# Second batch's softmax sums and joined maxima computed by PE, and the weights' sign written as a byte by GpSimd

## The chip, the cores and the metric

The kernel runs on one core of one Trainium2 chip. A core has five engines that run their own instruction streams side by side: PE (TensorE, matrix products into PSUM), DVE (VectorE, elementwise work, reductions, 32x32 transposes), ACT (ScalarE, functions such as exp and ln), POOL (GpSimd, elementwise work in SBUF, no PSUM) and SP (SyncE, which here only issues DMAs). The metric is the device time of one launch in microseconds (us); lower is better.

## The reference

Attention with 32 global and 512 local tokens for 8 batches of 8 heads (head size 64), and behind it a feed-forward layer on all 8 x 544 rows. Each local query sees the 32 global keys and the local keys at most 32 places away; each global query sees all keys.

```python
s_g = scale * np.matmul(q_g, k_all.transpose(0, 1, 3, 2))
out_g = np.matmul(sm(s_g), v_all)
mask = np.abs(pos[:, None] - pos[None, :]) <= window
s_ll = np.where(mask, scale * np.matmul(q_l, k_l.transpose(0, 1, 3, 2)), -1e9)
out_l = np.matmul(sm(np.concatenate([s_lg, s_ll], axis=-1)), v_all)
x = attn_out.transpose(0, 2, 1, 3).reshape(B * S, H * D)      # 4352 x 512
h = x @ w_in                                                   # 512 x 2048
g = np.maximum(h, 0.0) + np.log1p(np.exp(-np.abs(h)))
out = g @ w_out                                                # 2048 x 512
```

`sm` is the softmax: the row's maximum is subtracted, the exponentials are divided by their sum plus 1e-9. All inputs are fp32, but the weights come as 64-bit words: on the host the float32 array is viewed as `uint64` only, and the program gets them as pairs of 32-bit words, of which it works out a float32 value per pair.

## The kernel before

**Numbers of the feed-forward layer.** Every operand is split into two float32r halves (a rounded value and the rest), and each product is done three times (high x high, high x low, low x high), by `hpart` (h = x w_in, four pairs of heads j, 16 blocks f of 128 columns) and `opart` (o = g w_out). All products go through the helper `mm` (line 132), which chains them: PE executes them in the order in which the program writes them. `act` (lines 530 to 537) turns h into g: three ACT functions, a DVE instruction (L533) that reads the PSUM tile a last time, a rounded copy on ACT (L536, `gh`), the rest on POOL (L537, `gl`).

**Weights.** There are 16 blocks each of w_in and w_out. `load_w` brings a block as pairs of words, low and high. `abs_w` (L470, ACT) scales the value of the high word as a float, `bits_w` builds the float32 on DVE with three instructions: L477 shifts that left by three, L479 masks the sign out of the high word and ors it in, L482 shifts the low word right by 29 and ors. `halves_w` (L487 on ACT, L488 on POOL) splits it into two float32r tiles. Nine blocks are done during the first batch's attention, in which the order of DVE and ACT is written out by hand (`keep`, `note`): a block's three DVE instructions stand between a step's row maximum (L169, L170) and the inverse of its sums (L178, L179). The others follow in the next stage, each behind the latest joined maxima on DVE (`after(i, "maxima")`); `weights` takes one block whole before the next. Most of the temporary tiles of these steps share the tag "mb" with the attention's spread maxima, two buffers.

**Attention.** The first batch (m = 0 to 3, two heads each) is done by queries, in ten steps, before the feed-forward layer starts. All later batches go by keys: pair m computes score products with keys as rows (`scores`, two parts p, each into a two-bank PSUM tile), and each query's maximum and sum run across partitions. For the second batch (m = 4 to 7, `m < MPE`) PE adds the mask and ACT copies the scores (L310); later DVE does both (L312). DVE's transposing reduction L313 leaves for each 32-row block a column of maxima, and `gather` joins the four blocks: three POOL copies (L325) bring them to partitions 0 to 31, four DVE reductions and a copy (L328 to L332) join them by query, three more copies (L338) send them back. `probs` spreads the maxima by a DVE transpose (L346), POOL subtracts them in place (L355, L357), and ACT takes the exponential (L358). `sums` does the same with additions (L368, `gather`, L371 to L377), and `values` multiplies by the values on PE and by the inverse sums on DVE (L396).

**Order around the change.** A list of pieces, each with a place in the program, is mixed into the feed-forward layer's products: for pair m, scores at 12m and 12m+6 (with the maxima and exponentials behind the second), sums at 12m+14, values at 12m+21. In the first batch's products the 54 places from 54 to 108 are spread over the products by their count. Outside the hand-written part a planner orders each engine's instructions but PE's, by the program's order and estimated times.

**PSUM.** Tag "a" is one tile of two banks for scores, value products and the first batch's transposes; tag "h" is two banks for h; the rest holds o (before that, the first scores).

```python
ps.append((12 * m + 8 + LAG_Z, lambda m=m: sums(m)))      # LAG_Z = 6
def end(m):
    return 12 * m + 8 + LAG_V                             # LAG_V = 13
```

Of the kernel before, what the change touches and what calls it, by code (L numbers as in the profile page):

```python
# [35 lines left out]
LAG_V = 13  # L36
STEP = 3
# [26 lines left out]
def moe_over_global_local_attention(  # L64
# [27 lines left out]
    identf = pl.tile([P, P], F32, tag="e", name="identf", bufs=2)  # L92
    mask = const.tile([P, 2, 512], BF16, name="mask")
# [14 lines left out]
    def key_masks():  # L108
        near = mask[:, 1]
# [207 lines left out]
    def grid(t, start, *dims):  # L317
        base = t[0:32, start:start + 1]
        return bass.AP(base.tensor, base.offset, [list(base.ap[0])] + [list(d) for d in dims])
# [3 lines left out]
    def gather(mt, op):  # L323
        for a in range(1, 4):
            nc.gpsimd.tensor_copy(mt[0:32, GW * a:GW * a + GW], mt[32 * a:32 * a + 32, 0:GW])  # L325
        e0 = 4 * GW + 1
        for u, off in ((-1, 2), (2, 3)):
            nc.vector.tensor_reduce(grid(mt, e0 + u, (7, 6), (1, 2)), grid(mt, 4 + u - 2 * (u < 0), (12, 6), (1, 2), (off, 2), (GW, 4)), axis=AX.XY, op=op)  # L328
        nc.vector.tensor_reduce(grid(mt, e0 + 1, (7, 6), (4, 2)), grid(mt, 4 + 1, (12, 6), (7, 2), (GW, 4)), axis=AX.X, op=op)
        g = e0 + 42  # L330
        nc.vector.tensor_reduce(grid(mt, g, (1, 2)), grid(mt, 4 + 4, (36, 2), (12, 3), (3, 2), (GW, 4)), axis=AX.XYZ, op=op)
        nc.vector.tensor_copy(grid(mt, e0 + 4, (21, 2), (7, 3)), mt[0:32, g:g + 2].unsqueeze(2).to_broadcast([32, 2, 3]))  # L332
        return mt[:, e0:e0 + 42]

    def maxima(m):
        e = gather(st.pop(("mt", m)), ALU.max)
# [5 lines left out]
    def probs(m, p):  # L342
        s, e = st["s", m, p], st["e", m]
        k = QW[p] // 32
        mb = pl.tile([P, 2, 352], F32, tag="mb", name=f"mb{m}_{p}", bufs=2)
# [17 lines left out]

    def sums(m):
# [11 lines left out]
        rb = st["rb", m] = pl.tile([P, rows_of(608)], F32, tag="rb", name=f"rb{m}", bufs=1)[:, 0:608]  # L376
        nc.vector.transpose(rb.rearrange("p (s k) -> p s k", k=32), zr[:, 0:19].unsqueeze(2).to_broadcast([P, 19, 32]))  # L377

    def values(m):
# [3 lines left out]
        parts = ((0, 0, 0, 160, 0, 0), (1, 0, 160, 192, 0, 64), (2, 0, 352, 160, 0, 192), (2, 1, 0, 32, 0, 352), (3, 1, 32, 96, 0, 288),  # L383
                 (3, 1, 128, 96, 1, 0), (4, 1, 224, 192, 1, 32), (5, 1, 416, 96, 1, 128))
        seen = set()
        for c, p, o, w, bank, at in parts:
            for h in range(2):
                mm(ps[64 * h:64 * h + 64, bank, at:at + w], lhsT=vt[:, h, c], rhs=st["s", m, p][:, h, o:o + w],
                   start=(bank, h) not in seen, stop=(c, bank) in ((3, 0), (5, 1)), skip_group_check=True)
                seen.add((bank, h))  # L390
# [11 lines left out]
    def end(m):  # L402
        return 12 * m + 8 + LAG_V

    def pieces():
# [6 lines left out]
        for m in range(M0, M):  # L412
            for p in range(NPC):
# [3 lines left out]
                if p == 1:  # L417
                    fs.append(lambda m=m: maxima(m))
                    fs += [lambda m=m, q=q: probs(m, q) for q in range(NPC)]
                ps.append((12 * m + 6 * p, piece(*fs)))  # L420
            ps.append((12 * m + 8 + LAG_Z, lambda m=m: sums(m)))
# [43 lines left out]
    def abs_w(kind, k):  # L465
        if A_LO <= k < NF - A_UP:
            a = pl.tile([P, 512], I32, tag=f"{kind}{k + A_UP}", name=f"wbits{kind}{k}", bufs=1)
        else:
            a = pl.tile([P, 512], I32, tag="mb", name=f"wbits{kind}{k}", bufs=2)
        note("act", nc.scalar.mul(a.bitcast(F32), raws[kind, k][:, :, 1].bitcast(F32), DOWN))  # L470
        return a

    def bits_w(kind, k, a):
        t = raws.pop((kind, k))
        lo32, hi32 = t[:, :, 0], t[:, :, 1]

        i = nc.vector.tensor_scalar(a, a, 3, None, op0=ALU.logical_shift_left)  # L477
# [267 lines left out]
```

## Time and profile before

| | |
|---|---|
| median of 3 runs | 990.09 us (990.07 to 990.39) |
| profiled execution, its own time | 991.48 us |
| its span | 989.7 us |
| PE, busy share of the span | 946.2 us (96%) |
| DVE | 643.1 us (65%) |
| ACT | 492.6 us (50%) |
| POOL | 469.5 us (47%) |
| mean granted TensorE clock | 0.988 |

The span is what the profiler recorded of that one execution; its own time has some microseconds around it. Busy shares are means over the whole launch, in which the stages differ; a matmul's end is modelled, so a busy PE can still have small gaps. Rows of the profile give line, engine, operation, what is written and read, count, busy time and mean duration, and behind a bar how long the engine was idle before them and for whom it waited. A DMA is issued by SP or ACT and lands later by itself.

### The profile page before, as it was taken

What the parts mean: (1) busy time and instruction counts of PE and PEld (TensorE: products, weight loads), DVE (VectorE), ACT (ScalarE), POOL (GpSimd) and SP (SyncE); (2) the same over time, 40 slices, a digit from 0 to 9 for tenths busy, and PEclk for the clock granted to TensorE, in tenths of its full rate; (3) what the DMA queues carried; (4) which work ended last, traced back from release to release, by engine and by line L of the source; (5) the groups of instructions that cost most, each with busy time, mean ns of one, the idle gap of its engine ahead of it and who ended that gap; (6) DMA issues with size and microseconds to landing.
All of it is one profiled execution on the core that took longest, in us unless ns stands there. A gap on an engine that the chain in (4) does not pass through costs nothing.

```text
span 989.7 us, 14732 instructions
## 1 busy us (share of the span) xinstructions
PE 946.2 (96%) x5476; PEld 763.8 (77%) x5476; DVE 643.1 (65%) x1193; ACT 492.6 (50%) x811; POOL 469.5 (47%) x648
## 2 busy tenths in 40 slices
PE   6998598889999999999999999999999999999998
PEld 4776476668888788878887888878887888888896
DVE  5869898896667756786669666776668665411211
ACT  5756466544444544454445444454454445444453
POOL 4437776655445544444445544554445444322221
PEclk8998899999999999999999999999999999999999
DMA  9651331211112211121112111121112100100000
GB/s 357 231 188 46 122 111 57 65 66 41 47 47 69 69 47 46 48 74 47 47 37 72 47 47 47 66 71 47 47 33 88 32 17 1 65 1 1 10 35 22
DMA packets 30697, 64.60 MB, mean 65 GB/s; under 512 B 7328, under 2 KB 7840, under 8 KB 30624
## 3 DMA queue, kind: packets, MB, share of 16 engines
q1 hardware_dynamic: 29888, 63.32, 19.0%
q8 instruction: 43, 0.70, 0.3%
q10 hardware_dynamic: 736, 0.33, 0.2%
q14 instruction: 30, 0.25, 0.1%
HBM read 54.20 MB, written 9.44 MB: 64 GB/s over the span
## 4 chain that ended last, share of the span: by engine, by line
PE 67%; DVE 9%; POOL 4%; issue 3%; ACT 1%; DMA 1%; POOLq 0%; DVEq 0%; ACTq 0%
PE o L132 30%; PE h L132 29%; PE s_ps L132 5%; PE v_ps L132 4%; DVE xh L442 1%; DVE zt L368 1%; DVE xl L443 1%; POOL xl L443 1%; DVE mb L346 1%; POOL mt L325 1%; DVE s L312 1%; POOL s L355 1%; DVE xa L396 1%; DVE mt L332 0%; DVE e L533 0%
## 5 line engine op out<-in xcount | busy, mean ns | idle before, releaser
L132 PE MATMUL h<-xh,wi 128*128 128x512 f32 (+1 forms) x1152 | 341.9, 380 | 6.5 <-DVE e L533 5.8
L132 PE MATMUL o<-wo,gh 128*128 128x512 f32 x1088 | 344.8, 398 | 0.0
L537 POOL TENSOR_TENSOR gl<-e,gh 128x512 fp32r<-128x512 f32 x136 | 180.5, 1327 | 315.7 <-ACT gh L536 263.2
L132 PEld LDWEIGHTS h<-xh,wi 128*128 128x128 f32 x1152 | 211.1, 188 | 51.8 <-DVE e L533 8.9
L132 PEld LDWEIGHTS o<-wo,gh 128*128 128x128 f32 x1088 | 198.8, 188 | 46.0 <-issue 3.3
L533 DVE SCALAR_TENSOR_TENSOR e<-h,e 128x512 f32<-128x512 f32 x136 | 92.7, 682 | 210.1 <-ACT e L532 192.5
L132 PE MATMUL h<-xl,wi 128*128 128x512 f32 (+1 forms) x576 | 217.6, 378 | 0.9 <-DVE xl L443 0.9
L132 PE MATMUL o<-wo,gl 128*128 128x512 f32 x544 | 213.1, 392 | 0.2
L530 ACT ACTIVATE e<-h 128x512 f32<-128x512 f32 x136 | 81.0, 595 | 175.5 <-PE h L132 173.5
L536 ACT CAST gh<-e 128x512 fp32r<-128x512 f32 x136 | 84.5, 622 | 154.7 <-DVE e L533 154.5
L132 PEld LDWEIGHTS h<-xl,wi 128*128 128x128 f32 x576 | 108.4, 188 | 21.7 <-DVE xl L443 1.3
L355 POOL TENSOR_TENSOR s<-s,mb 128x640 f32<-128x640 f32 (+1 forms) x56 | 96.6, 1725 | 57.8 <-DVE mb L346 57.8
L132 PEld LDWEIGHTS o<-wo,gl 128*128 128x128 f32 x544 | 102.4, 188 | 23.2 <-POOL gl L537 1.1
L368 DVE TRANSPOSE_TENSOR_REDUCE zt<-s 128x32 f32<-128x1024 f32 x56 | 69.4, 1239 | 58.9 <-ACT s L358 58.7
L358 ACT ACTIVATE s<-s 128x1024 f32<-128x1024 f32 x56 | 59.4, 1061 | 83.5 <-POOL s L357 47.7
L532 ACT ACTIVATE e<-e,one 128x512 f32<-128x512 f32 x136 | 98.4, 723 | 4.3
L531 ACT ACTIVATE e<-e 128x512 f32<-128x512 f32 x136 | 85.9, 632 | 3.9
L313 DVE TRANSPOSE_TENSOR_REDUCE mt<-s 128x32 f32<-128x1024 f32 x56 | 68.9, 1231 | 3.7 <-ACT s L310 2.9
L132 PE MATMUL s_ps<-raw 64*128 64x192 f32 (+2 forms) x672 | 64.3, 325 | 0.6 <-issue 0.6
L132 PEld LDWEIGHTS v_ps<-s,v 128*64 128x64 f32 x896 | 49.4, 137 | 19.5 <-ACT s L310 6.5
L132 PE MATMUL v_ps<-s,v 128*64 128x96 f32 (+3 forms) x896 | 56.7, 280 | 7.3 <-ACT s L310 5.2
L132 PEld LDWEIGHTS s_ps<-raw 64*128 64x128 f32 x672 | 53.5, 192 | 11.6 <-issue 10.8
(147 smaller groups left out, 886.0 us busy)
## 6 DMA issues: line engine op xcount, KB each, us to landing
raw<-in_qk SPq DMA_DIRECT2D x32, 352.0 KB, 3.0
v<-in_v SPq DMA_DIRECT2D x28, 384.0 KB, 3.0
raw<-in_qk SPq DMA_DIRECT2D x28, 368.0 KB, 3.6
wiraw<-in_w_in SPq DMA_DIRECT2D x16, 512.0 KB, 8.5
woraw<-in_w_out SPq DMA_DIRECT2D x16, 512.0 KB, 7.4
out<-ot SPq DMA_DIRECT2D x32, 256.0 KB, 2.1
v<-in_v SPq DMA_DIRECT2D x4, 512.0 KB, 8.6
raw<-in_qk SPq DMA_DIRECT2D x4, 416.0 KB, 8.3
```

Of the source, the lines that this page charges most:

```text
L132: order["pe"] = after(nc.tensor.matmul(*a, **k), "pe").ins
L313: order["scores"] = nc.vector.tensor_reduce(windows(mt, 4 + 16 * p, 36, 2, 16), s.rearrange("p h (b k) -> p h b k", k=32), axis=AX.X, op=A ...
L355: nc.gpsimd.tensor_tensor(sw, sw, pairs(mb, 352, mo, md, w), op=ALU.subtract)
L358: nc.scalar.activation(s, s, AF.Exp, scale=0.125)
L368: nc.vector.tensor_reduce(windows(zt, 4 + 16 * p, 36, 2, 16), st["s", m, p].rearrange("p h (b k) -> p h b k", k=32), axis=AX.X, op=ALU.add ...
L443: (nc.vector if j % 2 else nc.gpsimd).tensor_tensor(lo, f(t), hi.bitcast(F32), op=ALU.subtract)
L530: nc.scalar.activation(e, ph, AF.Abs)
L531: nc.scalar.activation(e, e, AF.Exp, scale=-1.0)
L532: nc.scalar.activation(e, e, AF.Ln, bias=one)
L533: nc.vector.scalar_tensor_tensor(e, ph, 0.0, e, op0=ALU.max, op1=ALU.add)
L536: nc.scalar.copy(gh, e)
L537: nc.gpsimd.tensor_tensor(gl, e, gh.bitcast(F32), op=ALU.subtract)
```

## The change

Five edits. (1) The joined maxima of m = 4 to 7 come from four PE products of the block maxima with selection matrices (`quads`, each a row of four 32x32 identities), which put each block's maxima on all four partition groups in PSUM; `gather` then reduces from there on all 128 partitions, without the POOL copies and without L338. This is a piece of its own, two places after the second scores. (2) The sums of m = 4 to 7 are products of the exponentials with a matrix of ones, in the shapes of the value products, into a bank of tag "h" and the second half of the value tile's second bank; DVE transposes them out of PSUM, adds the global queries' parts, inverts and spreads them. (3) They stand in the values' piece, at 12m+15 and no more at 12m+21. (4) A weight's sign is written by POOL as one byte (128 where the value is negative, else 0) over the top byte of the low word, after DVE has shifted that word right by 29; one DVE instruction is then left behind ACT's scaling. (5) A block's shift, sign and scaling are begun one block ahead; tag "mb" has three buffers.

```diff
+    quads = const.tile([P, 4, P], F32, name="quads")
+    ones = const.tile([P, D], F32, name="ones")
     def key_masks():
+        nc.gpsimd.tensor_copy(quads.rearrange("p a (c k) -> p a c k", c=4),
+                              identf.rearrange("p (a k) -> p a k", a=4).unsqueeze(2).to_broadcast([P, 4, 4, 32]))
...
     def maxima(m):
+        mt = st.pop(("mt", m))
+        if m < MPE:
+            ps = ps_a.tile([P, 2, 512], F32, tag="a", name=f"m_ps{m}")[:, 0]
+            for a in range(4):
+                mm(ps[:, GW * a:GW * a + GW], lhsT=quads[:, a], rhs=mt[:, 0:GW], start=True, stop=True, skip_group_check=True)
+            st["e", m] = gather(mt, ALU.max, ps)
+            return
...
+    def weighted(m, banks, lhs, seen):
+        for c, p, o, w, bank, at in VPARTS:
+            for h in range(2):
+                mm(banks[bank][64 * h:64 * h + 64, at:at + w], lhsT=lhs(h, c), rhs=st["s", m, p][:, h, o:o + w], ...)
+    def sums_pe(m, zs):
+        z = pl.tile([P, rows_of(608)], F32, tag="mb", name=f"z{m}", bufs=3)[:, 0:608]
+        for t, at, w in ((zs[0], 0, 384), (zs[1], 384, 224)):
+            nc.vector.transpose(z[:, at:at + w], t[:, 0:w])
+        zr = pl.tile([P, ROW], F32, tag="zr", name=f"zr{m}", bufs=2)
+        nc.vector.tensor_scalar(zr[:, 0:19].unsqueeze(2), windows(z, 0, 32, 19, 1), 1e-9, None, op0=ALU.add)
+        nc.vector.tensor_reduce(zr[:, 19:20], windows(z, 128, 224, 3, 1).rearrange("p a b -> p b a"), axis=AX.X, op=ALU.add)
+        nc.vector.tensor_scalar(windows(zr, 4, 7, 3, 1), zr[:, 19:20].unsqueeze(1).to_broadcast([P, 3, 1]), 1e-9, None, op0=ALU.add)
+        nc.vector.reciprocal(zr[:, 0:19], zr[:, 0:19])
+        spread(m, zr)
...
     def values(m):
+        if m < MPE:
+            zs = (ps_h.tile([P, 512], F32, tag="h", name=f"z_ps{m}"), ps[:, 1, 256:512])
+            weighted(m, zs, lambda h, c: ones, set())
+        weighted(m, (ps[:, 0], ps[:, 1]), lambda h, c: vt[:, h, c], {(1, 0), (1, 1)} if m < MPE else set())
+        if m < MPE:
+            sums_pe(m, zs)
...
     def end(m):
-        return 12 * m + 8 + LAG_V
+        return 12 * m + (EARLY_V if m < MPE else 8 + LAG_V)
...
+                if m < MPE:
+                    if p:
+                        ps.append((12 * m + 6 + LAG_M, piece(*tail)))
...
+    def signs_w(kind, k):
+        t = raws[kind, k]
+        note("dve", i := nc.vector.tensor_scalar(t[:, :, 0], t[:, :, 0], 29, None, op0=ALU.logical_shift_right))
+        b = t.rearrange("p c w -> p (c w)").bitcast(mybir.dt.uint8).rearrange("p (c b) -> p c b", b=8)
+        nc.gpsimd.tensor_scalar(b[:, :, 3], t[:, :, 1].bitcast(F32), 0.0, 128.0, op0=ALU.is_lt, op1=ALU.mult)
+        return i
     def bits_w(kind, k, a):
-        i = nc.vector.tensor_scalar(a, a, 3, None, op0=ALU.logical_shift_left)
-        note("dve", i) if tight else after(i, "maxima")
-        note("dve", nc.vector.scalar_tensor_tensor(a, hi32, -0x80000000, a, op0=ALU.bitwise_and, op1=ALU.bitwise_or))
-        note("dve", nc.vector.scalar_tensor_tensor(r, lo32, 29, a, op0=ALU.logical_shift_right, op1=ALU.bitwise_or))
+        note("dve", nc.vector.scalar_tensor_tensor(r, a, 3, t[:, :, 0], op0=ALU.logical_shift_left, op1=ALU.bitwise_or))
+    def begin_w(kind, k):
+        if (kind, k) not in begun:
+            i = signs_w(kind, k)
+            if not tight:
+                after(i, "maxima")
+            begun[kind, k] = abs_w(kind, k)
+        return kind, k, begun[kind, k]
...
     def weights(upto):
+                begin_w(*order_w[wk[1]])
+                if wk[1] + 1 < len(order_w) and order_w[wk[1] + 1]:
+                    begin_w(*order_w[wk[1] + 1])
                 split_w(*order_w[wk[1]])
...
         if -1 <= k and wk[1] < W_PRE:
-            held = order_w[wk[1]]
-            held += (abs_w(*held),)
+            held = begin_w(*order_w[wk[1]])
```

LAG_M is 2 and EARLY_V is 15.

More of the change, by code (lines that the diff above doesn't have):

```diff
@@ L36 @@
 LAG_V = 13
+LAG_M = 2
+EARLY_V = 15
 STEP = 3
@@ L315, in scores, with grid, gather @@
         st["s", m, p] = s
-    def grid(t, start, *dims):
-        base = t[0:32, start:start + 1]
+    def grid(t, start, *dims, rows=32):
+        base = t[0:rows, start:start + 1]
         return bass.AP(base.tensor, base.offset, [list(base.ap[0])] + [list(d) for d in dims])
-    def gather(mt, op):
-        for a in range(1, 4):
-            nc.gpsimd.tensor_copy(mt[0:32, GW * a:GW * a + GW], mt[32 * a:32 * a + 32, 0:GW])
+    def gather(mt, op, src=None):
+        rows = P if src is not None else 32
+        if src is None:
+            src = mt
+            for a in range(1, 4):
+                nc.gpsimd.tensor_copy(mt[0:32, GW * a:GW * a + GW], mt[32 * a:32 * a + 32, 0:GW])
@@ L344, in probs @@
         k = QW[p] // 32
-        mb = pl.tile([P, 2, 352], F32, tag="mb", name=f"mb{m}_{p}", bufs=2)
+        mb = pl.tile([P, 2, 352], F32, tag="mb", name=f"mb{m}_{p}", bufs=3)
         nc.vector.transpose(mb[:, :, :QW[p]].rearrange("p h (s k) -> p h s k", k=32),
@@ L375, in sums @@
             nc.vector.reciprocal(zr[32 * a:32 * a + 32, 0:19], z[0:32, 21 * h:21 * h + 19])
-        rb = st["rb", m] = pl.tile([P, rows_of(608)], F32, tag="rb", name=f"rb{m}", bufs=1)[:, 0:608]
-        nc.vector.transpose(rb.rearrange("p (s k) -> p s k", k=32), zr[:, 0:19].unsqueeze(2).to_broadcast([P, 19, 32]))
+        spread(m, zr)
+    VPARTS = ((0, 0, 0, 160, 0, 0), (1, 0, 160, 192, 0, 64), (2, 0, 352, 160, 0, 192), (2, 1, 0, 32, 0, 352), (3, 1, 32, 96, 0, 288),
+              (3, 1, 128, 96, 1, 0), (4, 1, 224, 192, 1, 32), (5, 1, 416, 96, 1, 128))
+    def weighted(m, banks, lhs, seen):
+        for c, p, o, w, bank, at in VPARTS:
+            for h in range(2):
+                mm(banks[bank][64 * h:64 * h + 64, at:at + w], lhsT=lhs(h, c), rhs=st["s", m, p][:, h, o:o + w],
+                   start=(bank, h) not in seen, stop=(c, bank) in ((3, 0), (5, 1)), skip_group_check=True)
+                seen.add((bank, h))
+    def sums_pe(m, zs):
[7 more added lines that the diff above has]
+        nc.vector.reciprocal(zr[:, 0:19], zr[:, 0:19])
+        spread(m, zr)
     def values(m):
@@ L416, in pieces @@
                     fs.append(lambda m=m, p=p: load(m + 1, p))
[L417 to L421, printed above, removed]
+                tail = [lambda m=m: maxima(m)] + [lambda m=m, q=q: probs(m, q) for q in range(NPC)] if p else []
+                if m < MPE:
+                    if p:
+                        ps.append((12 * m + 6 + LAG_M, piece(*tail)))
+                    tail = []
+                ps.append((12 * m + 6 * p, piece(*fs, *tail)))
+            if m >= MPE:
+                ps.append((12 * m + 8 + LAG_Z, lambda m=m: sums(m)))
             fs = [lambda m=m: values(m)]
@@ L497, in output_banks @@
         return banks["o"]
-    one = const.tile([P, 1], F32, name="one")
-    nc.vector.memset(one, 1.0)
     def moe_items():
@@ L624, in moe_over_global_local_attention @@
     loads(W_PRE + 2)
-    first = end(H // 2 - 1) + STEP
+    first = 12 * (H // 2 - 1) + 8 + LAG_V + STEP
     pcs = pieces()
```

33 lines of the change are left out of this document (16 added, 17 removed).

## The prediction

> **What bounds the kernel now.** I read the page's head, then a table of busy time by stage (two stages and one slice; its first line names the columns), then the waits of PE in the stage that is not full.
>
> ```profile
> span 989.7 us, 14732 instructions
> ```
>
> ```profile
> core 0: us, PE busy (x) PEld busy (x) DVE busy (x) ACT busy (x) POOL busy (x), PEclk, DMA share, GB/s
> 59.00:216.00 157.00, 132.95 (x746) 102.52 (x741) 142.02 (x226) 88.32 (x143) 103.64 (x116) 0.96 0.28 97
> 216.00:324.00 108.00, 107.28 (x625) 86.44 (x625) 76.88 (x150) 51.62 (x79) 53.10 (x81) 1.00 0.17 53
> 80.00:90.00 10.00, 10.00 (x40) 7.20 (x40) 10.00 (x19) 5.34 (x11) 4.45 (x5) 0.69 0.02 3
> ```
>
> From 216 us on PE is full (107.28 of 108.0 us per batch) and nothing of the change runs there, so those 773 us stay. The change lives in the first 216 us: the first batch's attention (to about 59 us) and the stage from 59 to 216 us, in which the second batch's four head pairs (m = 4 to 7), most of the weight splitting and the first batch's expert products share the engines. There DVE is the fullest, 142.0 of 157.0 us (90%). PE is busy for 132.95 us at a mean clock of 0.96, which is 127.6 us of full-speed work; 29.4 us of the stage are not work: 24.05 us idle, 5.35 us lost to the slow clock. What PE waited for there:
>
> ```profile
> PE s_ps L132 <- DVE xa L396: 8.8, 2, 7.5
> PE v_ps L132 <- ACT s L310: 5.2, 3, 3.4
> PE o0g L132 <- ACT p0g1gh L254: 2.7, 1, 2.7
> PE v_ps L132 <- DVE s L312: 2.1, 1, 2.1
> PE h L132 <- DVE e L533: 1.3, 2, 1.2
> PE h L132 <- DVE xl L443: 0.9, 1, 0.9
> PE h L132 <- ACT yg L271: 0.7, 1, 0.7
> PE s_ps L132 <- issue: 0.6, 1, 0.6
> ```
>
> Most of it, 16.1 us (8.8, 5.2 and 2.1), hangs on the single two-bank tile of tag "a", which score products and value products take in turn: PE may not write it before ACT, or a late DVE, has read it. So a lighter DVE can be worth at most the 29.4 us, and every product that the change gives to PE is taken off that.
>
> **DVE's relief.** Rows of the same stage, by line:
>
> ```profile
> L479 DVE SCALAR_TENSOR_TENSOR wbitswo<-woraw,wbitswo 128x512 int32<-128x512 int32 x14 | 13.3, 954 | 0.2
> L479 DVE SCALAR_TENSOR_TENSOR wbitswi<-wiraw,wbitswi 128x512 int32<-128x512 int32 x10 | 9.8, 980 | 0.0
> L477 DVE TENSOR_SCALAR wbitswo<-wbitswo x14: 406/564/1543, 61.7 to 184.7; 128x512 int32<-128x512 int32 x14
> 59.00:216.00 157.00, 25.17 (x50) 4.85 (x19) 0.96 0.28 97
> L368 DVE TRANSPOSE_TENSOR_REDUCE zt<-s 128x32 f32<-128x1024 f32 x10 | 12.3, 1232 | 5.2 <-ACT s L358 5.0
> L338 DVE COPY mt<-mt 32x40 f32<-32x40 f32 x15 | 3.7, 248 | 0.3
> L377 DVE STREAM_TRANSPOSE rb<-zr 128x608 f32<-128x608 f32 x4 | 3.2, 802 | 0.0
> ```
>
> (The third row gives least, median and longest ns; the fourth is what writes or reads the tile zt: DVE 25.17 us in 50 instructions, POOL 4.85 in 19.) Per weight, three DVE instructions become two: the mask-and-or of L479 goes, the shift stays but reads every second word, the last one is the same two-input kind. That removes 13.3 + 9.8 = 23.1 us here. If the strided shift ran at half the rate it would add at most its 0.41 us once more, 9.7 us for 24; I take 0, since the contiguous shift's median is already above its least time. Per pair, the sums' twelve DVE instructions go: 25.17 less two reduces of m = 8 (2 x 1.23) is 22.7 us, and the three copies of L338, 12 x 0.25 = 3.0 us. In come two transposes of the new sums from PSUM, 384 and 224 elements, together the 608 of L377 (0.80 us) with one more start, and five small instructions; a start and a small instruction at L338's 0.25 us make 2.3 us a pair, 9.2 in all. DVE: 142.0 - 23.1 - 22.7 - 3.0 + 9.2 = 102.4 us, 65% of the stage, less than the 71% (76.88 of 108) at which the next stage keeps PE full.
>
> **GpSimd's load.** 24 of its 30 small gather copies go (7.5 us), 24 sign bytes come.
>
> ```profile
> L325 POOL COPY mt<-mt 32x76 f32<-32x76 f32 x15 | 4.8, 320 | 1.6 <-DVE mt L313 1.0
> L325 POOL COPY zt<-zt 32x76 f32<-32x76 f32 x15 | 4.6, 306 | 10.5 <-DVE zt L368 10.1
> masks.py:199 POOL TENSOR_SCALAR_AFFINE_SELECT identf<-identf 128x128 f32<-128x128 f32 x1 | 0.3, 294 | 0.0
> L101 POOL TENSOR_SCALAR_AFFINE_SELECT mask<-mask 128x32 bf16<-128x32 bf16 x2 | 0.4, 214 | 0.0
> L488 POOL TENSOR_TENSOR wo<-woraw,wo x13: 1294/1322/1795, 64.4 to 176.9; 128x512 fp32r<-128x512 f32 x13
> ```
>
> No row shows a write of single bytes. From below, the one-input affine selects give (294 - 214) / 96 = 0.83 ns an element, 0.61 us for 512; from above, the two-input subtract of the same size takes 1.29 us alone and 1.80 us at its longest. I take 0.8 us, nearer the one-input rows: POOL 103.6 - 7.5 + 19.2 = 115.3 us (110.7 to 139.3 at the ends). Building the four selection matrices once is one such copy, before POOL's first part in the attention; the waits for the first loads cover it, and without that cover it costs 0.6 us.
>
> The shift of L477 takes 406 ns at its shortest and 1543 at its longest, for the same shape. The Trainium skill ("SBUF — State Buffer", "Who interferes with whom") says that VectorE with two SBUF inputs, or in a two-port mode, and a GpSimd instruction that reads SBUF lock each other out for a whole instruction. By that rule, which would explain the long ones, each of the 24 added reads may hold one DVE instruction for its 0.8 us, and DVE would stand at 121.6 us and not 102.4, still below PE's sum but with more late stalls; it speaks for the second and third rival below.
>
> **PE's load.** Both the products with ones and the selections are new work on the engine that bounds the rest.
>
> ```profile
> 227.47 1.96 PE v_ps L132 x32
> 63.98 1.00 PE L132 MATMUL o0g<-p0g0gh,v 128*128 128x64 f32 x8
> ```
>
> The products with ones copy the shapes of the value products: 1.96 us a pair, 7.8 us. A pair's four selections are eight instructions with a full 128x128 fp32 weight load and 76 columns; the nearest row takes 1.00 us for eight with 64 columns: 4.0 us. PE's sum: 127.6 + 7.8 + 4.0 = 139.4 us, so 17.6 of the 29.4 us are left to win.
>
> **What PE will wait for.** PE's order is the order of the program. The selections stand two places (of 54 in the stage) after a pair's second score product, about 2 x 139.4 / 54 = 5.2 us of PE work, and need ACT's copy and DVE's L313 of that product. Now:
>
> ```profile
> 96.86 1.09 PE L132 MATMUL s_ps<-raw 64*128 64x192 f32 x12
> 108.88 1.23 DVE L313 TRANSPOSE_TENSOR_REDUCE mt<-s 128x32 f32<-128x1024 f32 x1
> 133.98 1.09 PE L132 MATMUL s_ps<-raw 64*128 64x192 f32 x12
> 141.53 1.20 DVE L313 TRANSPOSE_TENSOR_REDUCE mt<-s 128x32 f32<-128x1024 f32 x1
> 160.83 1.09 PE L132 MATMUL s_ps<-raw 64*128 64x192 f32 x12
> 172.16 1.23 DVE L313 TRANSPOSE_TENSOR_REDUCE mt<-s 128x32 f32<-128x1024 f32 x1
> 328.53 1.09 PE L132 MATMUL s_ps<-raw 64*128 64x192 f32 x12
> 331.61 1.25 DVE L313 TRANSPOSE_TENSOR_REDUCE mt<-s 128x32 f32<-128x1024 f32 x1
> ```
>
> From the product's end to L313's end it takes 12.2, 7.7 and 11.5 us for m = 5, 6, 7 (m = 4, at the stage's start, is left out), but 3.2 us in the full stage. At today's lags PE would stand still for 7.0 + 2.5 + 6.3 = 15.8 us, with everything in its queue behind it; at the full stage's lag not at all. With DVE at 65% I take a quarter, 4 us. The sums' tile takes one of the two banks of tag "h", so the next h waits until ACT and DVE (L533) have emptied the h before it. The longest such wait is 1.2 us now: 0 to 4.8 us over four pairs; I take 1, since output products lie between. The removed waits on xa and s (16.1 us) go with the earlier values and the lighter DVE. Of the others 2.2 us (xl, yg, issue) stay; the 2.7 us on p0g1gh and the slow clock behind it (0.31 x 10 us in the slice from 80) are ACT standing behind a late DVE, and I halve them: 2.9.
>
> Stage after: 139.4 + 4 + 1 + 2.2 + 2.9 = 149.5 us, 7.5 less.
>
> **The first stage loses.** DVE's order is fixed by hand there, and it has no spare place where the shift now stands:
>
> ```profile
> 29.05 0.69 DVE L213 COPY p_0gl<-t 96x512 f32<-96x512 f32 x1
> 29.66 1.08 DVE L169 TENSOR_REDUCE sums<-s 128x4 f32<-128x896 f32 x1
> 30.77 0.38 DVE L170 TENSOR_SCALAR sums<-sums 128x4 f32<-128x4 f32 x1
> 31.06 0.41 DVE L477 TENSOR_SCALAR wbitswi<-wbitswi 128x512 int32<-128x512 int32 x1
> 33.42 0.17 DVE L178 TENSOR_SCALAR sums<-sums 128x4 f32<-128x4 f32 x1 [0.49 <-ACT e L172]
> ```
>
> Today the weights' instructions lie between L170 and L178, where DVE would wait for ACT's exponentials anyway: taking one out wins nothing. The shift moves to between L213 and L169, which stand back to back. The rows are one of five steps in which DVE is gapless there; in the others it waits for PE after. 5 x 0.41 = 2.1 us. From below 0; from above 0.41 at nine weights and 0.4 more at each where POOL's byte delays L170 (0.38 here against 0.17 alone), 7.3 us.
>
> **Sum.** -7.5 + 2.1 = -5.4 us. It is made against the profiled execution, whose span is 989.7 of 991.5 us; the runs have a median of 990.09, and the same step taken off that gives 985 us.
>
> **The rivals.** *Full relief*: the new waits do not appear and the stage falls to PE's sum plus the 0.7 us of idle of the next one, 140.1: -16.9 + 2.1, 975 us. For it: the next stage is full with DVE at 71%. Against it: two new meetings of PE and DVE per pair. *GpSimd takes over as the bound*: at 1.80 us a byte write POOL has 139.3 us, and at the 90% that DVE reaches now that is 154 us, -3 + 2.1: 989 us, no change. For it: POOL already runs 66% and its subtracts feed both exponentials and gl. Against it: one-input rows are far cheaper. *PE stands at the selections* (the other side): if the copy and L313 stay as late as now, 139.4 + 15.8 + the 8.0 us of other waits kept whole + 2.1 = 165.3 us, +8.3: 998 us. It decides as soon as the selections wait more than some 9 us in all. For it: ACT's copy was late because ACT stood behind gh and the weights, whose count stays. Against it: the lag is 3.2 us once DVE is not full.
>
> **How the numbers follow.** What a measurement can tell from no change is 0.2%, 2.0 us. Forecast with its own range 979 to 988: 0.40; full relief: 0.13; GpSimd as bound, or new products and waits just eating the gain (988 to 992): 0.19; PE at the selections (992 to 1002): 0.28. So faster 0.53, same 0.19, slower 0.28. The range for 8 in 10 is 974 to 1000: it leaves out the floor's last microseconds and the slow end where the first stage also loses its 7.
>
> **What would show it.** Right: DVE below 110 us between 59 and 216 us, PE's waits on xa gone, L533 prompt after L532, the stage some 7 us shorter, the first stage about 2 longer. Wrong: selection products waiting for L313 over 2 us each; byte writes above 1.3 us; gl late with POOL above 85%; DVE standing at the weights' last instruction for a byte. If the first 59 us grow by more than 5 us, the moved shift was the larger term.

## The result and the profile after

The changed kernel takes 1020.85 us (median, 1019.59 to 1021.57) and the kernel before 990.08 us beside it: 3.1% slower, ratio 1.0309 (95% interval 1.0291 to 1.0327). The prediction said 985 us with a range of 974 to 1000; the time lies 21 us above that range. The profiled execution took 1019.59 us, 28.1 us more than the one of before.

The head of the page after, two of its lines:

```profile
span 1017.8 us, 14943 instructions
...
PE 965.6 (95%) x5629; PEld 781.6 (77%) x5636; DVE 600.8 (59%) x1125; ACT 494.7 (49%) x811; POOL 539.7 (53%) x653
```

PE idles 1017.8 - 965.6 = 52.2 us (before: 43.5 us) and is busy 19.4 us longer. VectorE was relieved as meant, from 643.1 to 600.8 us; GpSimd got 70.2 us more. Next, the busy time by stage of the kernel after: up to the first product of h, from there to a full PE, and one full batch.

```profile
core 0: us, PE busy (x) PEld busy (x) DVE busy (x) ACT busy (x) POOL busy (x), PEclk, DMA share, GB/s
0.00:78.80 78.80, 53.19 (x384) 41.38 (x385) 42.07 (x102) 37.99 (x109) 61.40 (x56) 0.89 0.50 190
78.80:236.00 157.20, 139.86 (x869) 110.85 (x874) 92.88 (x153) 83.61 (x132) 131.64 (x98) 0.92 0.28 93
236.00:344.00 108.00, 106.98 (x624) 86.18 (x623) 74.75 (x141) 52.33 (x79) 55.27 (x83) 1.00 0.17 53
```

The first products of h begin at 78.8 us and not at 59.2 us, as the rows of their group show, before and after (ns of one: least, median, longest; then first and last start):

```profile
L132 PE MATMUL h<-xh,wi x1152: 277/389/690, 59.2 to 976.4; 128*128 128x512 f32 x171, 128*128 128x256 f32 x21
L140 PE MATMUL h<-xh,wi x1152: 277/389/508, 78.8 to 1003.8; 128*128 128x512 f32 x171, 128*128 128x256 f32 x21
```

So the first stage, for which I had taken 2.1 us, lost 19.6 us, and all that comes behind it 28.1 - 19.6 = 8.5 us, where I had taken a gain of 7.5. From 236 us on PE is full as before. The group of the byte write, and the waits up to 260 us (who waited for whom: us in total, times, longest):

```profile
L522 POOL TENSOR_SCALAR wiraw<-wiraw x16: 2650/2700/3172, 15.9 to 186.0; 128x512 uint8<-128x512 f32 x16
L522 POOL TENSOR_SCALAR woraw<-woraw x16: 2637/2690/3663, 37.6 to 202.9; 128x512 uint8<-128x512 f32 x16
```

```profile
DVE woraw L528 <- POOL woraw L522: 16.3, 5, 8.8
DVE wiraw L528 <- POOL wiraw L522: 15.1, 7, 2.6
...
PE t L140 <- DVE p_0gl L221: 12.8, 3, 7.6
PE o L140 <- POOL gl L590: 8.6, 2, 4.9
```

A byte write takes 2.7 us as a rule (shortest 2.64, longest 3.66). VectorE's last instruction on a weight (L528) waits for it 31.4 us in all, 25.0 of them before 78.8 us; PE's transposes (`t`) wait for what is queued behind it on VectorE, and later the output products wait for `gl`, which stands behind byte writes on GpSimd. The longest of the waits, 8.8 us, from GpSimd's and VectorE's instructions in order of time (start, us):

```profile
37.56 2.83 POOL L522 TENSOR_SCALAR woraw<-woraw 128x512 uint8<-128x512 f32 x1
40.23 5.48 POOL L522 TENSOR_SCALAR wiraw<-wiraw 128x512 uint8<-128x512 f32 x2
45.54 1.03 POOL L193 TENSOR_TENSOR diag(2, 1)_414<-identf,sums 128x512 f32<-128x512 f32 x1
46.54 1.28 POOL L534 TENSOR_TENSOR wi<-wiraw,wi 128x512 fp32r<-128x512 f32 x1
47.79 5.13 POOL L522 TENSOR_SCALAR woraw<-woraw 128x512 uint8<-128x512 f32 x2
```

```profile
50.46 0.97 DVE L528 SCALAR_TENSOR_TENSOR woraw<-wbitswo,woraw 128x512 int32<-128x512 int32 x1 [8.76 <-POOL woraw L522]
```

GpSimd's order, which the planner makes, has three bytes (one `woraw`, two `wiraw`) of blocks that by their place are not among the first nine ahead of a step's `diag`. The byte that VectorE waits for is the first of the two that begin at 47.79 us. The hand-ordered VectorE stands from 41.7 us on: for the rest of those three, the `diag`, a subtract and its own byte. What the new products cost on PE, from its instructions in order of time (products with ones of one pair, selections of another):

```profile
186.35 1.37 PE L140 MATMUL z_ps<-s,ones 128*64 128x160 f32 x20
187.56 0.82 PE L140 MATMUL v_ps<-s,ones 128*64 128x96 f32 x12
...
89.11 1.01 PE L140 MATMUL m_ps<-mt,quads 128*128 128x76 f32 x8
```

### The profile page after: what moved, and what is told of

The parts are those of the page before. It is cut to its first block, busy times and chain, and to the rows that moved or that the text cites. A ratio compares the mean times of both kernels' runs of the same rounds, so it can differ in the third digit from the quotient of the medians.

```text
span 1017.8 us, 14943 instructions
## 1 busy us (share of the span) xinstructions
PE 965.6 (95%) x5629; PEld 781.6 (77%) x5636; DVE 600.8 (59%) x1125; ACT 494.7 (49%) x811; POOL 539.7 (53%) x653
## 4 chain that ended last, share of the span: by engine, by line
PE 72%; POOL 11%; DVE 10%; issue 4%; ACT 1%; DMA 1%; SPq 0%; POOLq 0%; ACTq 0%
PE o L140 31%; PE h L140 30%; PE s_ps L140 5%; PE v_ps L140 4%; POOL wiraw L522 3%; POOL woraw L522 2%; POOL wi L534 1%; DVE xh L487 1%; DVE xl L488 1%; DVE zt L392 1%; DMA wiraw<-in_w_in 1%; DVE mb L366 1%; POOL wo L534 1%; POOL s L375 1%; POOL xl L488 1%
## 5 line engine op out<-in xcount | busy, mean ns | idle before, releaser
L590 POOL TENSOR_TENSOR gl<-e,gh 128x512 fp32r<-128x512 f32 x136 | 176.4, 1297 | 314.7 <-ACT gh L589 262.3
L585 ACT ACTIVATE e<-e,ones 128x512 f32<-128x512 f32 x136 | 98.3, 722 | 4.3
L392 DVE TRANSPOSE_TENSOR_REDUCE zt<-s 128x32 f32<-128x1024 f32 x48 | 59.6, 1241 | 55.3 <-ACT s L378 55.3
L321 DVE TRANSPOSE_TENSOR_REDUCE mt<-s 128x32 f32<-128x1024 f32 x56 | 69.1, 1233 | 17.4 <-ACT s L318 16.3
L140 PE MATMUL s_ps<-raw 64*128 64x192 f32 (+2 forms) x672 | 63.5, 322 | 0.6 <-issue 0.4
L320 DVE TENSOR_TENSOR s<-s_ps,mask 128x1024 f32<-128x1024 f32 x48 | 58.2, 1212 | 6.6 <-PE s_ps L140 6.6
```

What stands on the lines that cost most here:

```text
L140: order["pe"] = after(nc.tensor.matmul(*a, **k), "pe").ins
L320: nc.vector.tensor_tensor(s, ps, mask[:, p].unsqueeze(1).to_broadcast([P, 2, 512]), op=ALU.add)
L321: order["scores"] = nc.vector.tensor_reduce(windows(mt, 4 + 16 * p, 36, 2, 16), s.rearrange("p h (b k) -> p h b k", k=32), axis=AX.X, op=A ...
L392: nc.vector.tensor_reduce(windows(zt, 4 + 16 * p, 36, 2, 16), st["s", m, p].rearrange("p h (b k) -> p h b k", k=32), axis=AX.X, op=ALU.add ...
L585: nc.scalar.activation(e, e, AF.Ln, bias=one)
L590: nc.gpsimd.tensor_tensor(gl, e, gh.bitcast(F32), op=ALU.subtract)
```

## The experiments

Each stands beside runs of the kernel before on the same chip (medians 990.0 to 990.6 us). Where a sentence gives the time from the first h product to the end, it is the profiled execution's span less the start of that product; before, 989.7 - 59.2 = 930.5 us. The theory at the start, A: the byte write's price is the loss, in the first stage as a wait of VectorE and in the second as GpSimd's load. Its rival, B: PE's new products and the early values are.

**Weights alone.** The diff's edits (4) and (5) on the kernel before.

> The kernel before with the weights' part of the change alone: the sign as a byte by GpSimd, the shift moved ahead, weights begun one block ahead; sums, maxima and values as before. Theory A (the byte write of 2.65 us is the loss): the first stage grows by about 19.6 us as in the changed kernel, and in the second stage GpSimd has 103.6 + 24 x 2.65 = 167 us of work for 157 us, so it grows by 10 to 20 us: 1020 to 1032 us. Theory B (TensorE's new products and the early values are the loss): 985 to 995 us.

1019.85 us, ratio 1.0293 (1.0278 to 1.0309): just under A's range, but not split as A says. The first h product stands at 69.1 us, 9.9 us later than before and not 19.6; from there on it takes 18.4 us more than before, with GpSimd busy 147.6 of the 166.9 us up to 236 us. Two of PE's waits up to 270 us:

```profile
PE o L132 <- POOL gl L548: 14.6, 2, 9.1
PE s_ps L132 <- DVE xa L396: 12.3, 1, 12.3
```

**Everything but the weights.** In the changed kernel:

```diff
+    def by_byte(kind, k):
+        return False
```

A weight for which `by_byte` is false is begun and built as before (L470, L477, L479, L482).

> The changed kernel with the weights as before (three VectorE instructions, no byte, nothing begun ahead); sums by products with ones, selections and early values stay. Theory A: the first stage is back at 59 us, and the second has VectorE at 142.0 - 22.7 - 3.0 + 9.2 = 125.5 us and TensorE at 139.4: 980 to 990 us. Theory B: 1010 to 1021 us.

1010.11 us, ratio 1.0184 (1.0163 to 1.0206): A falls as the only cause. Without any byte the change still costs 19.5 us. The two parts don't add up: 29.3 us for the weights alone, 19.5 for the rest alone, 30.8 together. PE's waits behind 59 us:

```profile
PE z_ps L140 <- DVE e L599: 11.0, 2, 7.4
PE o0g L140 <- ACT p0g1gh L262: 5.8, 1, 5.8
PE s_ps L140 <- DVE xa L438: 5.1, 2, 3.0
PE o0g L140 <- DVE p0g1gl L263: 2.2, 1, 2.2
```

The waits of before went down as predicted (on `xa` from 8.8 to 5.1 us, on `s` from 7.3 us to none), and others of the same size came: the products with ones wait until VectorE has read the h whose bank they take (L599 is `act`'s VectorE instruction here). PE's idle time is 46.5 us of the span of 1009.1, 3.0 more than before, and its busy time 16.4 us longer.

**The byte for some of the weights.** `by_byte` chooses between the two forms of a weight: the new one has the byte, the shift moved ahead and the early beginning.

```diff
+    def by_byte(kind, k):
+        return order_w.index((kind, k)) < W_PRE      # first nine; the other run has >=
```

> The changed kernel with the byte sign for the first nine weights alone (those of the hand-ordered first stage); the other 23 by three VectorE instructions as before. Theory A: the run without any byte plus what the first stage loses, some 15 to 20 us (three of the 19.6 came from bytes of later weights that the planner put ahead): 997 to 1010 us, and the first products of h begin at 74 to 79 us. A theory that the loss is GpSimd's load in the second stage alone: within 3 us of the run without any byte.

> The reverse: the first nine weights by three VectorE instructions, the other 23 with the byte. Theory A: the first stage is back near 59 us, the second is GpSimd's (about 96 + 23 x 2.65 = 157 us of work): the run without any byte plus 8 to 20 us, 990 to 1005 us. If the changed kernel's second stage lost its 8 us to a late start and not to GpSimd: within 3 us of the run without any byte.

First nine: 1022.25 us (ratio 1.0316, 1.0298 to 1.0334), first h product at 70.8 us, against 59.0 without any byte. The other 23: 1007.26 us (1.0166, 1.0151 to 1.0182), first h product at 63.9 us. So the new form of the nine weights in the hand-ordered stage costs 12.1 us against the run without any, nearly all of it before the first h product; A had said 15 to 20. The new form of the other 23 costs nothing net (2.9 us less): the first h product comes 4.9 us later (the planner puts some of their instructions into the first stage), and the rest takes 9.1 us less, as each also takes an instruction off VectorE. Beside the new sums and maxima A thus holds for the first stage and falls for the second. Beside the old ones, which leave GpSimd its gather copies and VectorE its sums, the second stage did lose 18.4 us (the weights alone).

**The parts on PE's side one by one**, with the weights as before, and VectorE's relief by itself.

```diff
-        note("dve", nc.vector.scalar_tensor_tensor(a, hi32, -0x80000000, a, op0=ALU.bitwise_and, op1=ALU.bitwise_or))
```

> The kernel before without the mask-and-or instruction of the weights (32 of them, 23.1 us of VectorE's time in the second stage), so the weights lose their sign; nothing else is touched. It measures what a lighter VectorE is worth by itself. My prediction's reasoning (TensorE's 24 us of idle time in the stage hang on a late VectorE): 975 to 983 us. The rival that the stage's idle time is in chains over several engines whose order the planner writes, and a lighter VectorE by itself wins little: 986 to 992 us.

977.35 us, ratio 0.9862 (0.9845 to 0.9878). The premise that a lighter VectorE is worth something holds: 28.6 us off it, 23.1 of them in the second stage and 5.5 in the first, gave 13.1 us.

The next three are the changed kernel with its other parts switched off: M_MAX and M_SUM bound the pairs that have selections and products with ones (M0 is 4, MPE 8), `by_byte` is false, and tag "mb" keeps three buffers.

```diff
+M_MAX = MPE
+M_SUM = M0
-EARLY_V = 15
+EARLY_V = 8 + LAG_V
```

> The kernel before with the maxima joined by selection products for four pairs, and nothing else of the change. By my terms: TensorE gets 4 x 0.86 = 3.4 us, waits some 1 us at the selections, VectorE and GpSimd lose some 3 and 5 us: 988 to 994 us. A rival that the selections are what makes the run without any byte 20 us slower: 1000 to 1010 us.

989.38 us, ratio 0.9984 (0.9975 to 0.9993): the selections cost nothing, though PE stood 5.0 us at one of them.

```diff
+M_MAX = M0
+M_SUM = MPE
-EARLY_V = 15
+EARLY_V = 8 + LAG_V
```

> The kernel before with the sums by products with ones for four pairs, values at their old place. By my terms: TensorE gets 7.8 us, VectorE loses 13.5 us: 988 to 996 us if the lighter VectorE gives back half. A rival that the bank which the sums take from the h products is what costs: 1000 to 1010 us, with the sums' products waiting for VectorE's last read of the h before.

1009.54 us, ratio 1.0187 (1.0171 to 1.0202): the products with ones alone lose as much as the run without any byte. The time is that of the rival with the bank, its wait is not: the products with ones stand 0.5 us for VectorE's last read of h, the next h products 9.1 us for it, and the next scores 14.9 us for `xa`.

```diff
+M_MAX = M0
+M_SUM = M0
```

EARLY_V stays 15.

> The kernel before with the values of four pairs six places earlier, right behind the sums on VectorE, and nothing else of the change. By my terms the waits of the next scores for the attention output go and new ones for the sums come: 986 to 994 us. A rival that the early place is what costs, since TensorE then stands at the values for ACT's exponential: 998 to 1008 us.

1002.23 us, ratio 1.0113 (1.0095 to 1.0131). The early place alone costs 11.8 us. The profile names the wait: PE stands 19.5 us, three times, for `xa`, so for VectorE, and not for ScalarE's exponential, which the rival named. The parts don't add up: 19.1 and 11.8 us alone, with the maxima 19.5 us together. With the sums ahead of it on VectorE the early place costs; with the products with ones and the selections it adds 0.6 us (1010.11 against 1009.54).

**Three causes and a price put to the test.**

```diff
-            zs = (ps_h.tile([P, 512], F32, tag="h", name=f"z_ps{m}"), ps[:, 1, 256:512])
+            zs = (ps[:, 1, 256:512], ps[:, 1, 256:512])      # columns taken modulo 64
```

> The run without any byte (1010 us), with the products with ones written over each other into the free columns of the values' own two banks, so that no bank is taken from the h products; the same products run, but the sums that come out aren't the rows' sums. If the bank is what costs: the 11.0 us that the sums' products stood for VectorE's last read of h go, with some 5 us of slow clock behind them: 992 to 1000 us. If the stall only moves to the next late VectorE instruction: 1004 to 1012 us.

1009.74 us, ratio 1.0194 (1.0179 to 1.0209). The wait named in the profile is gone and nothing is won. The first row of PE's waits behind 59 us shows where it went:

```profile
PE s_ps L140 <- DVE xa L439: 14.0, 3, 8.8
```

```diff
-        nc.gpsimd.tensor_scalar(b[:, :, 3], t[:, :, 1].bitcast(F32), 0.0, 128.0, op0=ALU.is_lt, op1=ALU.mult)
```

> The changed kernel without GpSimd's byte write and with all else of it, so the weights lose their sign: what the change would be worth if the byte cost nothing. If the byte's price is the only term that I had wrong: 975 to 988 us. If the products with ones cost some 20 us by themselves, as the run without any byte says, and the lighter VectorE gives 13 of them back: 992 to 1000 us.

999.14 us, ratio 1.0081 (1.0064 to 1.0098). The byte's price is 1020.85 - 999.14 = 21.7 us, and the rest of the change costs 9.1. Against the three VectorE instructions of before, the new form of the weights costs 1020.85 - 1010.11 = 10.7 us. The group of the h products (first and last start), and PE's waits behind 59 us:

```profile
L140 PE MATMUL h<-xh,wi x1152: 277/389/505, 64.1 to 984.4; 128*128 128x512 f32 x171, 128*128 128x256 f32 x21
```

```profile
PE o0g L140 <- ACT p0g1gh L262: 7.8, 1, 7.8
PE z_ps L140 <- DVE e L585: 4.1, 1, 4.1
PE o0g L140 <- DVE p0g1gl L263: 1.4, 1, 1.4
```

Even without the byte the first stage is 4.9 us longer; of the edits that touch it the moved shift and the earlier beginning are what is left, since it was 59.0 us with the weights as before. It was as long, 63.9 us, where only the later 23 weights had the new form, so the moved shift of the first nine need not be the reason; no run moves the shift alone. From the first h product on it takes 997.6 - 64.1 = 933.5 us, 3.0 more than before, and with the byte 1017.8 - 78.8 = 939.0. So the byte costs 78.8 - 64.1 = 14.7 us in the first stage and 5.5 behind it.

```diff
-LAG_M = 2
+LAG_M = 4      # maxima by selection alone
```

> The kernel before with the maxima joined by selection products for four pairs, the selections four places behind the scores where the changed kernel has two. With two, TensorE stood 5.0 us at one selection; if two more places cover that: 983 to 987 us. If the probabilities then come late for the values in its place: 988 to 995 us.

990.0 us, ratio 0.9999 (0.9989 to 1.0008): the later place gains nothing, and the selections now stand 8.4 us for `xa`, whose reading frees their tile.

```diff
+    for k in range(4):
+        nc.gpsimd.tensor_scalar(b8, s8, 0.0, 128.0, op0=ALU.is_lt, op1=ALU.mult)      # L705; the others in the same way
```

> The kernel before with rows of instructions behind its last output, which use none of its data for the result: GpSimd's byte write with its strides and without, the same operation to whole words, with one operation in place of two, a copy and the two-input subtract, four of each, while VectorE runs thirty two-input shifts and then four byte writes of its own. If the two operations set the byte write's 2.65 us: one operation takes half, whole words the same. If the stride or the byte output does: contiguous whole words take under 1.3 us. If the byte write locked VectorE out as the subtract does, VectorE's shift beside it would take over 2 us and not 0.69.

1067.34 us, with the rows of instructions behind the last output. The groups by line (ns: least, median, longest): VectorE's two-input shift; on GpSimd the byte write as in the change, the subtract, bytes in a row from strided words, bytes from words in a row, strided words from strided words, whole words in a row with both operations, with a multiply and an add, with a multiply alone, the strided byte write with the comparison alone.

```profile
L703 DVE SCALAR_TENSOR_TENSOR price_ddst<-price_dsrc,price_ddst x30: 692/694/1636, 989.1 to 1016.4; 128x512 int32<-128x512 int32 x30
L705 POOL TENSOR_SCALAR price_dst<-price_src x4: 2982/3130/3152, 989.6 to 999.1; 128x512 uint8<-128x512 f32 x4
L707 POOL TENSOR_TENSOR price_dst<-price_src x4: 1589/1590/1736, 1002.3 to 1007.5; 128x512 f32<-128x512 f32 x4
L709 POOL TENSOR_SCALAR price_dst<-price_src x4: 2266/2410/2921, 1009.2 to 1016.5; 128x512 uint8<-128x512 f32 x4
L711 POOL TENSOR_SCALAR price_dst<-price_src x4: 1920/1920/2099, 1019.5 to 1025.7; 128x512 uint8<-128x512 f32 x4
L713 POOL TENSOR_SCALAR price_dst<-price_src x4: 1962/1962/1963, 1027.7 to 1033.8; 128x512 f32<-128x512 f32 x4
L715 POOL TENSOR_SCALAR price_dst<-price_src x4: 1920/1921/1921, 1035.9 to 1041.9; 128x512 f32<-128x512 f32 x4
L717 POOL TENSOR_SCALAR price_dst<-price_src x4: 617/617/618, 1043.9 to 1046.0; 128x512 f32<-128x512 f32 x4
L719 POOL TENSOR_SCALAR price_dst<-price_src x4: 1487/1488/1500, 1046.7 to 1051.4; 128x512 f32<-128x512 f32 x4
L721 POOL TENSOR_SCALAR price_dst<-price_src x4: 2211/2212/2217, 1053.0 to 1059.9; 128x512 uint8<-128x512 f32 x4
```

None of the three accounts holds alone. The kind of operation weighs most: the same 512 words take 0.62 us with a multiply and an add and 1.92 with the comparison and the multiply. The byte output by itself adds nothing (L711 against L715) and the stride by itself 0.04 us (L713), but strided bytes take 0.7 us more than bytes in a row (L705 against L709, both beside a busy VectorE). Dropping the second operation leaves 2.21 us (L721, with VectorE idle).

**Why the products with ones cost 19 us.**

```diff
-            ps.append((12 * m + 8 + LAG_Z, lambda m=m: sums(m)))
+            ps.append((12 * m + 8 + LAG_Z, (lambda m=m: sums(m)) if m >= MPE else lambda m=m: no_sums(m)))   # rb = ones
```

> The kernel before without the sums of the second batch's four pairs (no instruction takes their place; the division is by a tile of ones). It takes 22.7 us off VectorE in the second stage and gives TensorE nothing. If a lighter VectorE is worth here what it was worth without the mask-and-or (13 us): 973 to 981 us. If the sums lay where VectorE's time sets nothing: 987 to 992 us.

986.9 us, ratio 0.9953 (0.9938 to 0.9967). Taking 22.7 us of sums off VectorE is worth 3.7 us; taking 28.6 us of mask-and-or off it was worth 13.1.

```diff
-        spread(m, zr)
+        nc.vector.transpose(z..., zr[:, 0:19]...)            # the inverse sums, spread but not used
+        nc.gpsimd.memset(st["rb", m], 1.0)                   # the division's tile
```

> The kernel with the sums by products with ones alone (values at their old place, 1009.5 us), where all of their instructions run but the division is by a tile of ones and so doesn't wait for them. If the loss is the chain from the products over seven VectorE instructions to the division, which frees the tile that the next scores wait for: 992 to 1000 us. If it is TensorE's added work and the bank that the sums take from h: 1004 to 1011 us.

1003.96 us, ratio 1.0136 (1.0119 to 1.0153), at the border of the two. The division that waits for the sums is worth 1009.54 - 1003.96 = 5.6 us; the added work itself, against the run without sums, 17.1. From the heads of the two pages, without sums (span 984.8 us) and with unused sums (1001.9 us):

```profile
PE 946.2 (96%) x5469; PEld 765.4 (78%) x5476; DVE 623.3 (63%) x1141; ACT 492.8 (50%) x811; POOL 467.2 (47%) x636
PE 959.6 (96%) x5597; PEld 776.9 (78%) x5604; DVE 636.5 (64%) x1169; ACT 492.7 (49%) x811; POOL 466.1 (47%) x637
```

PE's busy time grows by 13.4 us and its idle time by 3.7 (38.6 to 42.3). The products are at most 4 x (1.37 + 0.82) = 8.8 us of that; the rest, 4.6, fits the slow clock: taken microsecond by microsecond up to 300 us, PE's busy time times the part of the clock that was not granted grows from 9.8 to 16.1 us. The mean clock falls from 0.988 to 0.980 of full speed over the span.

**Where VectorE's time sets the end.** The run without the mask-and-or again, for a profile:

> The kernel before without the mask-and-or once more, for a profile: 977 us. If the gain is TensorE's idle time, of which the stage before has 24.1 us, some 10 us or more of it is gone, and the slow clock with it; if it is elsewhere, the idle time stays.

976.68 us (ratio 0.9854, 0.9835 to 0.9874). The span is 975.0 us, 14.7 less than before, PE is busy 943.9 us of it, and its idle time falls from 43.5 to 31.1 us: 12.4 of the 14.7 us are idle time, the rest busy time for the same products. The first h product stands at 57.1 us, so 2.1 us are won in the first stage.

Low bits moved down by ScalarE, without and with the maxima by selection:

```diff
+        note("act", nc.scalar.activation(t[:, :, 0], b[:, :, 3], AF.Copy, bias=-15.5 / 32, scale=1.0 / 32))
-        i = nc.vector.tensor_scalar(a, a, 3, None, op0=ALU.logical_shift_left)
```

> The kernel before with the weights' low bits moved down by ScalarE (a scaled copy of the low word's top byte, one more instruction for each weight) and not by VectorE, which keeps two of its three instructions. It takes VectorE's shift of 0.4 to 1.5 us off each weight, some 13 us of the second stage, at the place where 23 us were worth 14: 980 to 986 us. If ScalarE, with 32 x 0.67 us more, is late for the exponentials and copies instead: 990 to 996 us.

> The same with the maxima joined by selection products, the one part of the change that cost nothing: if the two gains add, 1 us less than the run with the low bits alone, 979 to 985 us; if ScalarE is late for the scores' copies, which the selections wait for: 988 to 996 us.

993.74 us (ratio 1.0034, 1.0021 to 1.0047) and 994.66 us (1.0043, 1.0026 to 1.006): slower, both. And without that shift and with nothing in its place:

```diff
-        i = nc.vector.tensor_scalar(a, a, 3, None, op0=ALU.logical_shift_left)
```

> The kernel before without VectorE's shift of the weights' high words and with nothing in its place, so the weights come out wrong; 17.6 us of VectorE's time in the second stage. If the weights' instructions on VectorE are worth 0.6 us each us, as those of the mask-and-or were: 978 to 983 us, and the run with the low bits on ScalarE lost this gain to ScalarE's added 0.67 us a weight. If only the mask-and-or was worth anything: 987 to 992 us.

981.6 us, ratio 0.9911 (0.9895 to 0.9928). The shift's groups in the second stage of before:

```profile
L477 DVE TENSOR_SCALAR wbitswo<-wbitswo 128x512 int32<-128x512 int32 x14 | 10.1, 734 | 0.2 <-ACT wbitswo L470 0.2
...
L477 DVE TENSOR_SCALAR wbitswi<-wbitswi 128x512 int32<-128x512 int32 x10 | 7.5, 748 | 0.0
```

So 10.1 + 7.5 = 17.6 us off VectorE in the second stage and 3.9 in the first, 21.4 in all, are worth 8.8 us. The run with the low bits on ScalarE, whose VectorE also has two instructions for each weight, takes 12.1 us longer than this one: its 32 ScalarE instructions of 0.68 us each take back more than was won.

The runs side by side; idle time is the span less PE's busy time, the clock the mean granted over the span:

| run | median, us | first h product | PE idle | PE busy | clock |
|---|---|---|---|---|---|
| before | 990.1 | 59.2 | 43.5 | 946.2 | 0.988 |
| after | 1020.85 | 78.8 | 52.2 | 965.6 | 0.978 |
| weights alone | 1019.85 | 69.1 | 63.5 | 954.5 | 0.975 |
| all but the weights | 1010.1 | 59.0 | 46.5 | 962.6 | 0.980 |
| after without the byte | 999.1 | 64.1 | 37.9 | 959.7 | 0.985 |
| products with ones alone | 1009.5 | 58.7 | 48.7 | 959.0 | 0.978 |
| early place alone | 1002.2 | 58.6 | 44.5 | 955.2 | 0.980 |
| maxima alone | 989.4 | 60.5 | 34.6 | 952.7 | 0.985 |
| no sums | 986.9 | 59.6 | 38.6 | 946.2 | 0.988 |
| no mask-and-or | 976.7 | 57.1 | 31.1 | 943.9 | 0.990 |

Of the kernels that leave nothing of the work out, none is faster than the one before by more than 0.2%; nearest is the one with the maxima by selection alone, at 0.9984.

## Why the prediction was wrong

**The step that failed most is the byte write's price.** The prediction took 0.8 us, "nearer the one-input rows", within 0.61 and 1.80; it measured 2.7 us, so the upper bound was wrong too. Both bounds came from instructions that do another operation (an affine select, a subtract), and the run of prices shows that the operation sets the time more than the number of inputs does: 1.92 us with one input here, 1.29 for the subtract with two that the prediction cites. Removing the byte gives back 21.7 us of the 36 us between forecast and result, and even without it the kernel is slower than before. The prediction's own sign for it, "byte writes above 1.3 us", came true, and so did "VectorE standing at the weights' last instruction for a byte".

**What the wait for it costs was left at nothing.** The prediction charged the moved shift and 0.4 us for delays, but no wait of L528 for GpSimd in the hand-ordered stage. VectorE stood there for eight of the nine weights, 25.0 us in all, and the stage lost 19.6 us. The term of 2.1 us (bounds 0 to 7.3) for the moved shift was small but within its bounds, since the stage is 4.9 us longer without the byte. The prediction's sign that the moved shift was the larger term, a first stage longer by more than 5 us, came and misled: the byte was.

**GpSimd as the bound of the second stage**, the rival at 989 us, had the load about right (131.6 of 157.2 us from the first h product to 236 us; 115.3 forecast, 139.3 in the rival) and the place wrong: beside the rest of the change the new form of the later 23 weights cost nothing net, that of the first nine 12.1 us. GpSimd cost most where VectorE's fixed order waits for it. As the bound of the second stage it did appear with the weights alone, at 18.4 us.

**VectorE's relief was sized rightly and valued wrongly.** The 102.4 us forecast for VectorE in the stage came out as 92.9 us between the first h product and 236 us. But the sum took waits of 16.1 us off PE as if any VectorE time were worth the same. It isn't: 0.46 us for each us of mask-and-or (13.1 of 28.6), 0.41 for each us of the shift (8.8 of 21.4), 0.16 for each us of the sums (3.7 of 22.7). Without the byte the stage shows both sides: of the waits on `xa` and `s` 1.0 us is left, and waits of 13.3 us stand on `p0g1gh`, `p0g1gl` and on h's last reader, where the stage before had 4.0. For the idle time and the slow clock of the stage the prediction's sum leaves 10.1 us of 29.4; in the 157 us behind the first h product PE is idle 14.7 us without the byte and busy 142.3 us at a mean clock of 0.93, which loses some 10 us more. This is the step that failed in the second stage.

**PE's load was right in work and wrong in time.** Products with ones: 2.19 us a pair against 1.96 taken; selections 1.01 against 1.00. In all 12.8 us against 11.8. PE's busy time grew by 13.5 us without the byte and by 19.4 with it, and the mean clock fell (0.985 and 0.978 after 0.988). Microsecond by microsecond up to 300 us, the busy time lost to the slow clock is 8.2 us before, 12.0 without the byte and 16.0 with it: stalls cost a second time, in slow clock. The prediction counted on less slow clock than before.

**The slower rival, PE standing at the selections, fell**: the wait was 0.3 us with the change. So the outcome was on that rival's side, and beyond it, by another mechanism. The maxima alone gave 989.4 us.

**What stays open.** Why 8.8 us of products cost 17 us is shown only in its parts: about 9 us of work, 3.7 of idle time, the rest slow clock. Why the parts of the change cost less together (30.8 us) than apart (29.3 and 19.5) is not shown either; GpSimd's and VectorE's load in the second stage, which the new sums and maxima lighten, is the likely reason. Which stall brings the slow clock, and whether the planner's order on the other engines or the products themselves set it, no run told apart: taking away the wait that the profile named first moved it to the next.

## What to carry to other kernels

Price an instruction that the trace doesn't have by its operation as well as by its inputs and size, and measure it alone before putting 32 of them where another engine, ordered by hand, waits for each. Time taken off an engine is worth what the chain at that place makes of it: here 0.46 us per us at one place and 0.16 at another, on the same engine in the same kernel. Work added to the bounding engine can cost more than its own time: here 8.8 us of products cost 17.1, with stalls and slow clock. And measure the parts of a change apart and together: here they don't add up.

## What the hardware showed that I had not expected

**GpSimd's instruction with a number or two has its price by the operation**: a multiply and an add take 0.62 us for 512 words, a multiply alone 1.49, a comparison and a multiply 1.92.

**The byte write doesn't lock VectorE out, the subtract does.** VectorE's two-input shifts beside byte writes and beside subtracts, in the run of prices (the stretch, its length, busy time with the count; the rest is PE's clock, DMA share and GB/s):

```profile
989.70:1002.20 12.50, 11.99 (x16) 0.50 0.00 0
1002.40:1009.00 6.60, 6.46 (x5) 0.50 0.00 0
```

Beside byte writes 16 shifts fit into 12.5 us, beside subtracts 5 into 6.6. Each shift beside a subtract took 1.63 us or a little more; beside a byte write the first took 1.0 us and the others 0.69. The rule of the Trainium skill that the prediction weighed ("SBUF — State Buffer", "Who interferes with whom") agrees with the subtract and not with the byte write, though both read SBUF: a byte write held one shift up by 0.3 us, not for its whole 3.1 us.

**Long stalls slowed PE's clock inside them and behind them.** PE around the 7.4 us wait in the run with all but the weights (the stretch, its length, PE's busy time with its count, the granted clock, then DMA share and GB/s):

```profile
135.30:142.70 7.40, 0.00 (x0) 0.78 0.23 92
142.70:146.30 3.60, 3.57 (x32) 0.50 0.00 0
146.30:152.00 5.70, 5.70 (x53) 1.00 0.21 69
```

The 3.6 us of products behind the stall ran at half speed, after a clock of 1.00 in the 7.3 us ahead of it: 1.8 us more, on top of the 7.4. In the run without the byte the eight products `o0g` behind the wait of 7.8 us took 1.97 us, in the changed kernel behind one of 2.1 us 1.10.
